# First batch of an attention and two-layer kernel: transposing unnormalized probabilities and scaling the product by spread reciprocal sums

## The chip, the cores and the metric

The kernel runs on one core of a Trainium2 chip. The metric is the device time of one execution in microseconds, the median of several; lower is better. A change of 0.2% (about 2.4 us here) is taken as the least that a measurement can tell from no change.

## What is computed

Attention over 4 batches of 12 heads, 448 positions, head size 64, with RMS-normalized q and k; its output, as 1792 tokens of 768 values, runs through two layers (768 to 2048 and back, twice).

```python
q_n, k_n = (rmsnorm(q, g_q), rmsnorm(k, g_k))
scores = scale * np.matmul(q_n, k_n.transpose(0, 1, 3, 2))
scores = scores - np.max(scores, axis=-1, keepdims=True)
attn = np.exp(scores)
attn = attn / (np.sum(attn, axis=-1, keepdims=True) + 1e-09)
return np.matmul(attn, v).astype(np.float32)
...
h = x @ w_in
g = h * (1.0 / (1.0 + np.exp(-1.702 * h)))
return (g @ w_out).astype(np.float32)
...
h = x @ w_in
g = np.maximum(h, 0.0) + alpha * np.minimum(h, 0.0)
return (g @ w_out).astype(np.float32)
```

The weight matrices arrive as 64-bit floats, read as pairs of 32-bit words; the other inputs have 32 bits. Most products are made of three fp16 products of a high and a low half each; in the first batch the product of probabilities and values is made in fp32 instead.

## The kernel before, in words

Two heads make a pair P, so a batch has 6 pairs, and a pair has 4 units u (three of 2 x 64 query rows for both heads, the last of 64 rows). `attention` walks over units with a lag: for each it computes the scores (`scores`, tile `sp`, six fp16 matmuls, then the row maximum `nm` on VectorE), the exponentials and their sums (`exponent`, tiles `pr` and `sm`), one step later `high`, two steps later `low`, and every second unit, four steps later, the product with the values (`values`, tile `xp`).

In the first batch (`u < 4 * NP`) `high` takes the reciprocal of the sums and makes with ScalarE for each of the unit's one or two row sets a diagonal matrix `dg` that holds them. `low` multiplies each 128-column piece of `pr` with `dg` on TensorE in fp32, which transposes and normalizes in one step (tile `tp` in PSUM), and ScalarE copies it to SBUF (`ptf`). `values` then multiplies `ptf` with the raw fp32 values `v`:

```python
dg = att_p.tile([128, 2, 128], F32, tag="ph", name="dg", bufs=PHB)
nc.scalar.activation(out=dg[:, i], in_=identf, func=AF.Copy, scale=sm[:, i:i + 1])
nc.tensor.matmul(out=tp[:, c, i], lhsT=pr[i][:, o:o + 128], rhs=ph[:, i], start=True, stop=True)
```

In the later batches the probabilities are normalized as two fp16 halves (`ph`, lines 505 and 531) and transposed by DMA; none of that is touched.

The order of the program: `first_pairs` runs the first two units of each pair of batch 0 (12 units, 256 of the 448 columns of x), while `w1i_steps` builds the first weight matrix from its words. Then `first_x` splits these 256 columns into halves, and the second two units of each pair run (12 units, 192 columns), interleaved with `first_in` on the first 256 columns (tile `hp`, line 651) and with `w1o_steps` for the second weight matrix. Then `first_moe1` runs `first_in` on the other 192 columns and `moe1_out` (tile `yp`, line 721), with batch 1's attention in between, and `moe1(1)` follows (line 698). Within this the tile framework's scheduler decides each engine's final order; engines run their instructions in that order and wait on semaphores. All DMAs are issued from SyncE's queue (SP), also in a fixed order. PSUM tiles `tp`, `hp`, `yp`, `pm` share three buffers of the pool `ps_m`; `xp` has one buffer of its own.

Lines named below: 393 to 410 and 424 normalize a pair's q and k, 429 transposes it by DMA (`t<-hl`), 148 to 165 and 179 to 180 build weights, 128 and 129 send a maximum through DRAM and back to all partitions (`line`, `row`), 307 and 308 read v for its largest value, 570 copies `xp` to `xraw`.

Of the kernel before, what the change touches and what calls it, by code (L numbers as in the profile page):

```python
# [9 lines left out]
F32 = mybir.dt.float32  # L10
# [3 lines left out]
AF = mybir.ActivationFunctionType  # L14
ALU = mybir.AluOpType
AX = mybir.AxisListType.X

EXP_MASK = 0x7F800000
EV = (True, True)
VN = 8  # L20
D1 = 2
RAW0 = 5
# [14 lines left out]
SQB = 2  # L37
HLB = 1
PHB = 3
# [18 lines left out]
def attention_moe_kernel(  # L58
# [17 lines left out]
    nc = tc.nc  # L76
    B, H, S, D = q.shape
# [4 lines left out]
    NP = H // 2  # L82
# [3 lines left out]
    NX = NX_  # L86

    const = ctx.enter_context(tc.tile_pool(name="const", bufs=1))
    big = ctx.enter_context(tc.tile_pool(name="big", bufs=1))
    dram = ctx.enter_context(tc.tile_pool(name="dram", bufs=1, space=bass.MemoryType.DRAM))  # L90
    small = ctx.enter_context(tc.tile_pool(name="small", bufs=2))
    work = ctx.enter_context(tc.tile_pool(name="work", bufs=2))
    ps_m = ctx.enter_context(tc.tile_pool(name="ps_m", bufs=3, space=bass.MemoryType.PSUM))
# [6 lines left out]
    identf = const.tile([128, 128], F32, name="identf")  # L100
# [37 lines left out]
    def split(dst, src, scale):  # L138

        nc.scalar.activation(out=dst[0], in_=src, func=AF.Copy, scale=scale)  # L140
        nc.vector.scalar_tensor_tensor(  # L141
            out=dst[1], in0=src, scalar=scale, in1=dst[0], op0=ALU.mult, op1=ALU.subtract
        )
# [116 lines left out]
    scales = {}  # L260
    loads = {}
    w1i = big.tile([128, KD, 2, FF], F16, tag="w", name="w1i", bufs=2)
# [5 lines left out]
    att_p = att.enter_context(tc.tile_pool(name="att_p", bufs=2))  # L268
# [6 lines left out]
    av = const.tile([128, B], F32, name="av")  # L275
# [170 lines left out]
    probs = {}  # L446
    pts = {}
    xs = {}
    xraw = {}
# [5 lines left out]
    FIRST = 256  # L455
    first_sc = const.tile([128, KD], F32, name="first_sc")

    def unit(u):

        P, r = divmod(u, 4)  # L460
        return (P, *UNITS[r])

    def scores(u):
# [15 lines left out]
        nc.scalar.activation(out=nm[:, 0:n], in_=nm[:, 0:n], func=AF.Copy, scale=c_s)  # L479
        probs[u] = (sp, nm, n)  # L480

    def exponent(u):
        sp, nm, n = probs[u]
        pr = [att_p.tile([128, S], F32, tag="p", name="pr", bufs=4) for _ in range(n)]
        sm = small.tile([128, 2], F32, tag="sm", name="sm", bufs=4)
        for i in range(n):
            nc.scalar.activation(  # L487
                out=pr[i], in_=sp[:, i, 0:S], func=AF.Exp, bias=nm[:, i:i + 1], scale=c_s, accum_out=sm[:, i:i + 1]
            )
        sm = sm[:, 0:n]  # L490
        nc.scalar.activation(out=sm, in_=sm, func=AF.Copy, scale=2.0 ** -14, bias=1e-9 * 2.0 ** -14)
        probs[u] = (pr, sm)

    def high(u):
        pr, sm = probs[u]
        nc.vector.reciprocal(out=sm, in_=sm)  # L496
        if u < 4 * NP:
            dg = att_p.tile([128, 2, 128], F32, tag="ph", name="dg", bufs=PHB)
            for i in range(len(pr)):
                nc.scalar.activation(out=dg[:, i], in_=identf, func=AF.Copy, scale=sm[:, i:i + 1])  # L500
            probs[u] = (pr, sm, dg)
            return
        ph = att_p.tile([128, 2, 2 * S], F16, tag="ph", name="ph", bufs=PHB)
        for i in range(len(pr)):
            nc.scalar.activation(out=ph[:, i, 0:S], in_=pr[i], func=AF.Copy, scale=sm[:, i:i + 1])  # L505
        probs[u] = (pr, sm, ph)

    def low(u):
        P, half, cols, place = unit(u)
        pr, sm, ph = probs.pop(u)  # L510
        n = len(pr)
        if u < 4 * NP:
            if (P, half) not in pts:
                pts[P, half] = att_p.tile([128, NV, 512], F32, tag="pt", name="ptf")
            for h in range(2):
                tp = ps_m.tile([128, 2, n, 128], F32, tag="m", name="tp")
                for c in range(2):
                    o = min(128 * (2 * h + c), S - 128)
                    for i in range(n):
                        nc.tensor.matmul(out=tp[:, c, i], lhsT=pr[i][:, o:o + 128], rhs=ph[:, i], start=True, stop=True)  # L520
                d = cols[1] - cols[0]
                to = pts[P, half][:, 2 * h:2 * h + 2, 0:2 * d].rearrange("p c (i t) -> p c i t", i=2)
                to = to[:, :, :, cols[0]:cols[0] + 64 * n]
                src = tp if n == 2 else tp.rearrange("p c n (i t) -> p c (n i) t", i=2)
                if EV[h]:
                    nc.scalar.activation(out=to, in_=src, func=AF.Copy)  # L526
                else:
                    nc.vector.tensor_copy(out=to, in_=src)
            return
        for i in range(n):  # L530
            nc.vector.scalar_tensor_tensor(  # L531
                out=ph[:, i, S:2 * S], in0=pr[i], scalar=sm[:, i:i + 1], in1=ph[:, i, 0:S], op0=ALU.mult, op1=ALU.subtract
            )
        if (P, half) not in pts:
            pts[P, half] = att_p.tile([128, 7, 512], F16, tag="pt", name="pt")
        for i in range(2):
            nc.sync.dma_start_transpose(  # L537
                out=pts[P, half][:, :, cols[i]:cols[i] + 64 * n], in_=ph[:, i] if n == 2 else ph[64 * i:64 * i + 64, 0]
            )

    def values(P, half):
        b, p = divmod(P, NP)
        vs = preps[P][1]
        pt = pts.pop((P, half))
        if half == 0 or b == 0:
            xps[P] = ps_x.tile([128, S], F32, tag="x", name="xp")
        xp = xps[P]
        if b == 0:
            steps = [(c, c, slice(64 if c == 3 else 0, 128)) for c in range(NV)]
        else:  # L550
            steps = [(c, c, slice(0, 128)) for c in range(7)] + [(c + 7, c, slice(0, 128)) for c in range(4)]
        parts = PARTS[half]
        for group in (parts,) if b else [(part,) for part in parts]:
            for i, (c, kc, ks) in enumerate(steps):
                for j, o, t, n in group:
                    nc.tensor.matmul(  # L556
                        out=xp[64 * j:64 * j + 64, t:t + n],
                        lhsT=vs[ks, j, c],
                        rhs=pt[ks, kc, o:o + n],
                        start=(i == 0),  # L560
                        stop=(i == len(steps) - 1),
                    )
        if b and half == 0:
            xs[b, p] = big.tile([128, 2, S], F16, tag="x", name="x", bufs=NX)
        elif b:
            x = xs[b, p]
            split((x[:, 0], x[:, 1]), xp, scales["w1i"][1][:, p:p + 1])
        elif half == 0:
            xraw[p] = big.tile([128, S], F32, tag="x", name="xraw", bufs=NX)
            nc.scalar.activation(out=xraw[p][:, 0:FIRST], in_=xp[:, 0:FIRST], func=AF.Copy)  # L570
        else:
            first_split(p, xp, slice(FIRST, S))

    def first_split(p, src, cols):
        x = xs[0, p]
        split((x[:, 0, cols], x[:, 1, cols]), src[:, cols], first_sc[:, p:p + 1])

    def first_x():
        nc.vector.tensor_scalar(out=first_sc, in0=scales["w1i"][1], scalar1=av[:, 0:1], scalar2=None, op0=ALU.mult)
        for p in range(NP):  # L580
            xs[0, p] = big.tile([128, 2, S], F16, tag="x", name="x", bufs=NX)
            first_split(p, xraw[p], slice(0, FIRST))
# [3 lines left out]
    def attention(us):  # L586

        for i in range(len(us) + LAG):
            if 0 < i <= len(us):
                high(us[i - 1])  # L590
            if i < len(us):
                scores(us[i])
                exponent(us[i])
            if 2 <= i <= len(us) + 1:
                low(us[i - 2])
            if i >= LAG and us[i - LAG] % 2 == 1:
                values(us[i - LAG] // 4, us[i - LAG] % 4 // 2)
            yield
# [304 lines left out]
    sums = {}  # L903
# [171 lines left out]
    if True:  # L1075
# [42 lines left out]
        for _ in w1i_steps:  # L1118
            pass
        v_scales(0, v0)  # L1120
        first_x()
        moe1_scales(0)
        for P in range(NP, NP + 2):
# [75 lines left out]
```

## Time and profile before

| | |
|---|---|
| time, median of 3 runs | 1196.87 us (1195.72 to 1196.92) |
| span of the profiled execution (first to last instruction) | 1199.3 us |
| TensorE matmul busy | 1086.5 us (91%) |
| VectorE busy | 822.6 us (69%) |
| ScalarE busy | 692.2 us (58%) |
| GpSimd busy | 80.1 us (7%) |
| mean granted TensorE clock | 0.970 |

The span is what the profile has as the profiled execution's own time; it stands 2.4 us above the median of the runs. Busy shares are averages over stages with different limits, so they have to be read stage by stage: the first hp matmul (line 651, 256 columns) starts at 140.5 us, the first of 192 columns at 222.1, the first yp at 289.7 and the first of batch 1's hp (line 698) at 367.1. A busy TensorE is not at its peak: where the granted clock is low the same matmul lasts longer.

### The profile page before, as it was taken

To read this page: it belongs to the slowest core of one execution; us is meant where nothing else is said; L and a number is where in the kernel's file an instruction comes from. 1 tells how busy PE (TensorE), PEld (TensorE's weight loads), DVE (VectorE), ACT (ScalarE), POOL (GpSimd) and SP (SyncE) were. 2 spreads that over 40 slices of the span, in tenths; PEclk is the share of its full clock that TensorE was granted. 3 is DMA by queue.
4 is the path that set the end of the run, shared out by engine and by line. 5 is a ranking of instruction groups with operands and counts; after the bars stand their busy time and mean duration, and the time that the engine had idled before them with its cause. 6 is when DMAs were issued, how large, how long until landed. Compare 5 with 4: busy or idle time off the path is not lost.

```text
span 1199.3 us, 18528 instructions
## 1 busy us (share of the span) xinstructions
PE 1086.5 (91%) x6826; PEld 612.5 (51%) x6826; DVE 822.6 (69%) x1445; ACT 692.2 (58%) x1425; POOL 80.1 (7%) x200
## 2 busy tenths in 40 slices
PE   0567899878998998999998999999999999999998
PEld 0335566655544444544554545544444467666665
DVE  6988889989567786457752677489995422977351
ACT  3877788877477776568852445346555422655220
POOL 3111000352101101010000000000000000000000
PEclk9887899978999999999998999999999999999999
DMA  7973555578587775645562741275614423353111
GB/s 216 272 175 109 144 159 148 114 157 171 117 152 143 139 152 118 149 97 115 106 142 57 263 139 51 78 262 176 219 71 149 141 75 126 97 161 109 34 27 33
DMA packets 267403, 160.82 MB, mean 134 GB/s; under 512 B 188592, under 2 KB 250672, under 8 KB 267312
## 3 DMA queue, kind: packets, MB, share of 16 engines
q1 hardware_dynamic: 267312, 159.64, 51.6%
q8 instruction: 53, 0.87, 0.3%
q14 instruction: 38, 0.31, 0.1%
HBM read 92.22 MB, written 25.69 MB: 98 GB/s over the span
## 4 chain that ended last, share of the span: by engine, by line
PE 44%; DVE 19%; ACT 14%; DMA 11%; issue 6%; SPq 4%; POOL 2%; ACTq 0%; DVEq 0%; POOLq 0%
PE op L983 16%; PE h L823 8%; PE yp L721 6%; PE hp L698 4%; ACT pr L487 4%; PE xp L556 4%; DVE ph L531 3%; PE hp L651 3%; DVE nm L478 3%; PE tp L520 3%; DMA t<-hl 2%; DMA yr<-y_dram 2%; ACT ph L505 2%; SPq L537 1%; PE sp L473 1%
## 5 line engine op out<-in xcount | busy, mean ns | idle before, releaser
L721 PE MATMUL yp<-g,w1o 128*128 128x448 f16 x1152 | 227.0, 355 | 4.3 <-ACT g L140 1.8
L823 PE MATMUL h<-x,w2i 128*128 128x512 f16 (+1 forms) x1152 | 219.3, 352 | 4.2 <-DVE pos L829 2.2
L698 PE MATMUL hp<-x,w1i 128*128 128x448 f16 x864 | 169.3, 353 | 2.6 <-DVE t L707 2.1
L721 PEld LDWEIGHTS <-w1o 128*128 128x128 f16 x1152 | 110.9, 98 | 116.6 <-issue 17.4
L823 PEld LDWEIGHTS <-w2i 128*128 128x128 f16 x1152 | 112.6, 98 | 109.9 <-issue 5.5
L698 PEld LDWEIGHTS <-w1i 128*128 128x128 f16 x864 | 82.2, 98 | 84.7 <-issue 10.4
L487 ACT ACTIVATE pr<-sp,nm,c_s 128x448 f32<-128x448 f32 x168 | 120.3, 719 | 4.4 <-PE tp L520 1.6
L531 DVE SCALAR_TENSOR_TENSOR ph<-pr,sm,ph 128x448 f16<-128x448 f32 x126 | 89.0, 731 | 20.3 <-ACT ph L505 20.3
L478 DVE TENSOR_REDUCE nm<-sp 128x2 f32<-128x896 f32 x96 | 92.3, 963 | 5.7 <-PE sp L473 5.7
L828 ACT ACTIVATE pos<-h,sign 128x512 f32<-128x512 f32 (+1 forms) x64 | 40.0, 627 | 86.6 <-PE h L823 80.2
L505 ACT ACTIVATE ph<-pr,sm 128x448 f16<-128x448 f32 x126 | 78.0, 660 | 18.9 <-DVE sm L496 18.8
L983 PEld LDWEIGHTS <-even 128*128 128x128 f16 x672 | 65.7, 98 | 43.4
L829 DVE SCALAR_TENSOR_TENSOR pos<-h,slope,pos 128x512 f32<-128x512 f32 (+1 forms) x64 | 43.4, 679 | 59.3 <-ACT pos L828 59.3
L473 PE MATMUL sp<-t 64*128 64x448 f16 (+1 forms) x480 | 62.2, 365 | 18.1 <-ACT pr L487 13.7
L651 PE MATMUL hp<-x,w1i 128*128 128x256 f16 (+1 forms) x576 | 66.0, 274 | 8.9 <-ACT ptf L526 3.3
L479 ACT ACTIVATE nm<-nm,c_s 128x2 f32<-128x2 f32 x96 | 27.7, 291 | 70.0 <-DVE nm L478 70.0
L520 PE MATMUL tp<-dg,pr 128*128 128x128 f32 x336 | 54.3, 322 | 14.1 <-ACT dg L500 14.1
L983 PEld LDWEIGHTS <-odd 128*128 128x128 f16 x504 | 49.3, 98 | 32.6
L651 PEld LDWEIGHTS <-w1i 128*128 128x128 f16 x576 | 55.4, 104 | 19.0 <-issue 14.9
L556 PE MATMUL xp<-pt,vs 128*64 128x256 f16 (+1 forms) x792 | 52.0, 279 | 12.7 <-DVE x L141 7.6
L983 PE MATMUL op<-w2lo,even 128*128 128x384 f16 x384 | 63.4, 326 | 0.0
L520 PEld LDWEIGHTS tp<-dg,pr 128*128 128x128 f32 x336 | 49.1, 230 | 23.5 <-ACT dg L500 15.9
(204 smaller groups left out, 1553.5 us busy)
## 6 DMA issues: line engine op xcount, KB each, us to landing
g<-in_moe_w_in_dram SPq DMA_DIRECT2D x24, 512.0 KB, 5.1
g<-in_moe_w_out_dram SPq DMA_DIRECT2D x32, 384.0 KB, 4.0
w2raw<-in_moe_w_in_dram SPq DMA_DIRECT2D x24, 512.0 KB, 5.7
w2raw<-in_moe_w_out_dram SPq DMA_DIRECT2D x16, 768.0 KB, 6.6
g_dram<-pos SPq DMA_DIRECT2D x48, 256.0 KB, 2.0
gp<-g_dram SPq DMA_DIRECT2D x8, 1024.0 KB, 6.7
odd<-g_dram SPq DMA_DIRECT2D x6, 1024.0 KB, 5.6
y_dram<-y SPq DMA_DIRECT2D x24, 224.0 KB, 2.3
```

What stands on the lines that cost most here:

```text
L473: nc.tensor.matmul(out=sp[:, j, 0:S] if n == 2 else sp[ds, 0, 0:S], lhsT=qt[ds] if n == 2 else qt[ds, 64:128], rhs=kt[ds, 0:S], start=(i = ...
L478: nc.vector.tensor_reduce(out=nm[:, 0:n], in_=sp[:, 0:n, 0:S], op=ALU.max, axis=AX, negate=True)
L487: nc.scalar.activation(out=pr[i], in_=sp[:, i, 0:S], func=AF.Exp, bias=nm[:, i:i + 1], scale=c_s, accum_out=sm[:, i:i + 1])
L505: nc.scalar.activation(out=ph[:, i, 0:S], in_=pr[i], func=AF.Copy, scale=sm[:, i:i + 1])
L520: nc.tensor.matmul(out=tp[:, c, i], lhsT=pr[i][:, o:o + 128], rhs=ph[:, i], start=True, stop=True)
L531: nc.vector.scalar_tensor_tensor(out=ph[:, i, S:2 * S], in0=pr[i], scalar=sm[:, i:i + 1], in1=ph[:, i, 0:S], op0=ALU.mult, op1=ALU.subtract)
L556: nc.tensor.matmul(out=xp[64 * j:64 * j + 64, t:t + n], lhsT=vs[ks, j, c], rhs=pt[ks, kc, o:o + n], start=(i == 0), stop=(i == len(steps) ...
L651: nc.tensor.matmul(out=ps, lhsT=w1i[:, kk, e, m * 128:(m + 1) * 128], rhs=xs[0, kk][:, f, cols], start=(i == 0), stop=(i == 3 * KD - 1))
L698: nc.tensor.matmul(out=ps, lhsT=w1i[:, kk, e, m * 128:(m + 1) * 128], rhs=x[:, f], start=(n == 0), stop=(n == 3 * KD - 1))
L721: nc.tensor.matmul(out=ps, lhsT=w1o[:, m, e, j * 128:(j + 1) * 128], rhs=g[:, m, f], start=(n == 0), stop=(n == 3 * KF - 1))
L823: nc.tensor.matmul(out=ps, lhsT=w2i[:, kk, e, m * 128:(m + 1) * 128], rhs=x2[kk][:, f], start=(c == 0), stop=(c == 3 * KD - 1))
L983: nc.tensor.matmul(out=ps, lhsT=ops[:, o, m, f], rhs=rhs[:, e], start=(c == 0), stop=(c == 3 * KH - 1))
```

## The change

In the first batch `exponent` keeps the sums of two units side by side in one tile `sums`, and after the second adds 1e-9 and takes the reciprocal on VectorE; the scaling of the sums on ScalarE and the diagonal matrices are gone. `low` transposes `pr` as it is with TensorE's transpose against the identity. After the second unit `spread_sums` multiplies the reciprocals, broadcast over 64 columns, with the identity (fp32), which gives them along the free axis and over the 64 partitions of each head (tile `rp`); ScalarE copies that to SBUF (`own`, in the first half the tile `xraw` itself). `values` multiplies its product in PSUM with `own` on VectorE. For the second half the split into halves then reads SBUF.

```diff
+        if u < 4 * NP:
+            if u % 2 == 0:
+                sums_of[P, half] = small.tile([128, 4], F32, tag="sums", name="sums", bufs=3)
+            sm = sums_of[P, half][:, 2 * (u % 2):2 * (u % 2) + n]
...
-        nc.scalar.activation(out=sm, in_=sm, func=AF.Copy, scale=2.0 ** -14, bias=1e-9 * 2.0 ** -14)
+        if u >= 4 * NP:
+            nc.scalar.activation(out=sm, in_=sm, func=AF.Copy, scale=2.0 ** -14, bias=1e-9 * 2.0 ** -14)
+        elif u % 2:
+            sm = sums_of[P, half][:, 0:2 + n]
+            nc.vector.tensor_scalar(out=sm, in0=sm, scalar1=1e-9, scalar2=None, op0=ALU.add)
+            nc.vector.reciprocal(out=sm, in_=sm)
...
+    def spread_sums(P, half):
+        rs = sums_of.pop((P, half))
+        rp = ps_m.tile([128, 256], F32, tag="m", name="rp")
+        for h in range(2):
+            hs = slice(64 * h, 64 * h + 64)
+            for r in range(2):
+                if r and half:
+                    nc.tensor.matmul(
+                        out=rp[hs, 128:192], lhsT=rs[hs, 2:3].to_broadcast([64, 64]), rhs=identf[hs, hs], start=True, stop=True
+                    )
+                else:
+                    nc.tensor.matmul(
+                        out=rp[hs, 128 * r:128 * r + 128], lhsT=rs[:, 2 * r + h:2 * r + h + 1].to_broadcast([128, 64]),
+                        rhs=identf, start=True, stop=True
+                    )
+        if half:
+            own = att_p.tile([128, S - FIRST], F32, tag="sq", name="own", bufs=SQB)
+        else:
+            xraw[P] = big.tile([128, S], F32, tag="x", name="xraw", bufs=NX)
+            own = xraw[P][:, 0:FIRST]
+        nc.scalar.activation(out=own, in_=rp[:, 0:S - FIRST] if half else rp, func=AF.Copy)
+        spread[P, half] = own
...
-        if u < 4 * NP:
-            dg = att_p.tile([128, 2, 128], F32, tag="ph", name="dg", bufs=PHB)
-            for i in range(len(pr)):
-                nc.scalar.activation(out=dg[:, i], in_=identf, func=AF.Copy, scale=sm[:, i:i + 1])
-            probs[u] = (pr, sm, dg)
-            return
...
-                        nc.tensor.matmul(out=tp[:, c, i], lhsT=pr[i][:, o:o + 128], rhs=ph[:, i], start=True, stop=True)
+                        nc.tensor.transpose(out=tp[:, c, i], in_=pr[i][:, o:o + 128], identity=identf)
...
+            if u % 2:
+                spread_sums(P, half)
             return
...
-            xraw[p] = big.tile([128, S], F32, tag="x", name="xraw", bufs=NX)
-            nc.scalar.activation(out=xraw[p][:, 0:FIRST], in_=xp[:, 0:FIRST], func=AF.Copy)
+            own = spread.pop((P, 0))
+            nc.vector.tensor_tensor(out=own, in0=xp[:, 0:FIRST], in1=own, op=ALU.mult)
         else:
-            first_split(p, xp, slice(FIRST, S))
+            own = spread.pop((P, 1))
+            cols = slice(FIRST, S)
+            nc.vector.scalar_tensor_tensor(
+                out=own, in0=xp[:, cols], scalar=first_sc[:, p:p + 1], in1=own, op0=ALU.mult, op1=ALU.mult
+            )
+            x = xs[0, p]
+            nc.scalar.activation(out=x[:, 0, cols], in_=own, func=AF.Copy)
+            nc.vector.tensor_tensor(out=x[:, 1, cols], in0=own, in1=x[:, 0, cols], op=ALU.subtract)
```

The scheduler puts much of the first 370 us into another order. Three places follow; the lines of the changed kernel are its own (there 495 is the exponential, 147 the step of line 148, 556 the copy to ptf, 526 the copy of rp).

ScalarE at the second and third unit, before and then changed (`w1i` and `g_139` are weights and their words):

```order
L487 ACTIVATE pr,sm<-sp,nm,c_s 128x448 x2
L500 ACTIVATE dg<-identf,sm 128x128 x2
L148 ACTIVATE w1i<-g_139 128x512
L423 ACTIVATE hl<-qk 128x896
L491 ACTIVATE sm<-sm 128x2
L391 ACTIVATE sq<-qk 128x448 x2
L148 ACTIVATE w1i<-g_139 128x512
L479 ACTIVATE nm<-nm,c_s 128x2
L526 ACTIVATE ptf<-tp 128x4x128
```

```order
L147 ACTIVATE w1i<-g_139 128x512 x2
L556 ACTIVATE ptf<-tp 128x4x128
L478 ACTIVATE nm<-nm,c_s 128x2
L556 ACTIVATE ptf<-tp 128x4x128
L178 ACTIVATE w1i<-w1i,inv_w1i 128x2048
L495 ACTIVATE pr,sums<-sp,nm,c_s 128x448 x2
```

The first copy to `ptf` stood behind the second unit's exponentials and the diagonals; it now stands ahead of the second unit's exponentials.

SyncE's queue where the last pair of batch 0 is transposed (`t_548` before, `t_538` changed), before and then changed:

```order
L223 DMA g_139<-in_moe_w_in_dram 128x1024 x2
L128 DMA line_7466<-am 128x1
L129 DMA row<-line_7466 128x128
L223 DMA g_139<-in_moe_w_out_dram 128x4x192
L429 DMA_TRANSPOSE t_548<-hl 128x14x128
L307 DMA vst<-in_v_dram 128x336 x4
L223 DMA g_139<-in_moe_w_out_dram 128x4x192
L307 DMA vst<-in_v_dram 128x336 x4
L223 DMA g_139<-in_moe_w_out_dram 128x4x192 x18
L429 DMA_TRANSPOSE t_2017<-hl 128x14x128
```

```order
L222 DMA g_139<-in_moe_w_in_dram 128x1024
L428 DMA_TRANSPOSE t_538<-hl 128x14x128
L222 DMA g_139<-in_moe_w_in_dram 128x1024
L306 DMA vst<-in_v_dram 128x336 x2
L127 DMA line_7448<-am 128x1
L128 DMA row<-line_7448 128x128
L222 DMA g_139<-in_moe_w_out_dram 128x4x192
L306 DMA vst<-in_v_dram 128x336 x2
L222 DMA g_139<-in_moe_w_out_dram 128x4x192
L306 DMA vst<-in_v_dram 128x336 x4
L222 DMA g_139<-in_moe_w_out_dram 128x4x192 x30
L440 DMA vs<-vs 64x2x192
```

The transpose of the last pair passed the send of the maximum `am`; the first transpose of batch 1 (`t_2017` before) now stands behind all loads of the second weight matrix.

VectorE where the first pair's product is taken out of PSUM in the changed kernel (before, ScalarE did that, line 570):

```order
L164 SCALAR_TENSOR_TENSOR w1i<-g_139,w1i 128x512 x3
L602 TENSOR_TENSOR xraw<-xp,xraw 128x256
L423 TENSOR_TENSOR hl<-qk,hl 128x896
L295 TENSOR_REDUCE vone<-v_95 128x1
L392 TENSOR_REDUCE ss<-sq 128x7
L477 TENSOR_REDUCE nm<-sp 128x2
```

The multiplication by `own` stands on VectorE ahead of the third pair's normalization and the next row maximum.

## Rows read from the trace of the kernel before

**Rows 1.** Busy time by stretch: length, then each engine's busy us and (instructions), clock, DMA

```profile
core 0: us, PE busy (x) PEld busy (x) DVE busy (x) ACT busy (x) POOL busy (x), PEclk, DMA share, GB/s
...
30.00:140.50 110.50, 76.80 (x402) 50.06 (x403) 95.53 (x180) 84.50 (x198) 14.11 (x42) 0.85 0.65 179
140.50:222.10 81.60, 78.20 (x580) 55.45 (x579) 72.96 (x164) 68.75 (x173) 1.37 (x1) 1.00 0.61 151
222.10:289.70 67.60, 49.03 (x493) 38.37 (x493) 60.51 (x120) 55.44 (x134) 29.86 (x41) 0.85 0.72 138
289.70:367.10 77.40, 72.56 (x488) 36.90 (x488) 49.49 (x92) 46.11 (x111) 8.63 (x29) 0.98 0.69 144
```

**Rows 2.** Waits from 30 to 140.5 us: waiter, releaser, us in total, times, longest

```profile
PE tp L520 <- ACT dg L500: 14.1, 5, 4.6
ACT xraw L570 <- PE xp L556: 13.4, 6, 5.9
...
PE sp L473 <- ACT w1i L148: 8.6, 1, 8.6
...
DVE g L164 <- ACT g L148: 5.4, 1, 5.4
...
PE sp L473 <- DMA t<-hl: 4.5, 1, 4.5
...
DVE vcol L308 <- DMA vst<-in_v_dram: 2.4, 1, 2.4
...
DVE a L134 <- DMA row<-line: 1.7, 1, 1.7
```

**Rows 3.** SyncE's queue in order of time: start, us, issue

```profile
89.99 0.33 SPq L128 DMA_DIRECT2D line<-am  x1
97.92 0.33 SPq L129 DMA_DIRECT2D row<-line  x1
...
98.82 3.78 SPq L429 DMA_TRANSPOSE t<-hl  x1
```

**Rows 4.** Groups of equal instructions, 0 to 367.1 us: busy us, mean ns, idle before

```profile
L500 ACT ACTIVATE dg<-identf,sm 128x128 f32<-128x128 f32 x42 | 14.5, 397 | 0.5 <-DVE rm_w1i L105 0.5
...
L491 ACT ACTIVATE sm<-sm 128x2 f32<-128x2 f32 x38 | 7.7, 203 | 0.2
...
L663 DVE SCALAR_TENSOR_TENSOR g<-t,hp 128x256 f32<-128x256 f32 x16 | 6.4, 412 | 2.0 <-ACT t L662 1.5 <-DMA g<-in_moe_w_out_dram 0.5
...
L140 ACT ACTIVATE x<-xp,first_sc 128x192 f16<-128x192 f32 x6 | 2.6, 425 | 2.5 <-PE xp L556 2.5
...
L663 DVE SCALAR_TENSOR_TENSOR g<-t,hp 128x192 f32<-128x192 f32 x5 | 1.7, 340 | 0.0
```

**Rows 5.** The same view, the instructions of normalizing a pair and the row maximum

```profile
L478 DVE TENSOR_REDUCE nm<-sp 128x2 f32<-128x896 f32 x39 | 42.1, 1080 | 5.7 <-PE sp L473 5.7
...
L393 DVE TENSOR_REDUCE ss<-sq 128x7 f32<-128x448 f32 x36 | 21.1, 611 | 12.6 <-ACT sq L391 12.6
...
L410 DVE TENSOR_TENSOR qk<-qk,rs 128x896 f32<-128x896 f32 x12 | 12.6, 1087 | 9.0 <-POOL rs L404 8.8
...
L424 DVE TENSOR_TENSOR hl<-qk,hl 128x896 f16<-128x896 f32 x11 | 11.9, 1082 | 0.6 <-ACT hl L423 0.6
...
L409 DVE TENSOR_TENSOR qk<-qk,gs 128x512 f32<-128x512 f32 x14 | 9.6, 684 | 0.0
```

**Rows 6.** TensorE in order of time: start, us, instructions merged

```profile
47.16 3.78 PE L520 MATMUL tp<-dg,pr 128*128 128x128 f32 x16 [4.65 <-ACT dg L500]
...
56.63 2.05 PE L520 MATMUL tp<-dg,pr 128*128 128x128 f32 x16
...
165.42 2.14 PE L651 MATMUL hp<-x,w1i 128*128 128x256 f16 x18
167.49 0.74 PE L473 MATMUL sp<-t 64*128 64x448 f16 x6
```

**Rows 7.** Busy time of the instructions on tile tp, second stretch: length, PE, PEld, ACT

```profile
140.50:222.10 81.60, 18.39 (x128) 15.58 (x128) 10.30 (x22) 1.00 0.61 151
```

More of the change, by code (lines that the diff above doesn't have):

```diff
@@ L18 @@
 EXP_MASK = 0x7F800000
-EV = (True, True)
 VN = 8
@@ L480, in scores @@
         probs[u] = (sp, nm, n)
+    sums_of = {}
+    spread = {}
     def exponent(u):
         sp, nm, n = probs[u]
+        P, half, _, _ = unit(u)
         pr = [att_p.tile([128, S], F32, tag="p", name="pr", bufs=4) for _ in range(n)]
-        sm = small.tile([128, 2], F32, tag="sm", name="sm", bufs=4)
+        if u < 4 * NP:
[3 more added lines that the diff above has]
+        else:
+            sm = small.tile([128, 2], F32, tag="sm", name="sm", bufs=4)[:, 0:n]
         for i in range(n):
@@ L489, in exponent @@
             )
-        sm = sm[:, 0:n]
-        nc.scalar.activation(out=sm, in_=sm, func=AF.Copy, scale=2.0 ** -14, bias=1e-9 * 2.0 ** -14)
-        probs[u] = (pr, sm)
+        if u >= 4 * NP:
[4 more added lines that the diff above has]
+            nc.vector.reciprocal(out=sm, in_=sm)
+        probs[u] = (pr, sm)
+    def spread_sums(P, half):
[15 more added lines that the diff above has]
+            own = att_p.tile([128, S - FIRST], F32, tag="sq", name="own", bufs=SQB)
+        else:
+            xraw[P] = big.tile([128, S], F32, tag="x", name="xraw", bufs=NX)
+            own = xraw[P][:, 0:FIRST]
+        nc.scalar.activation(out=own, in_=rp[:, 0:S - FIRST] if half else rp, func=AF.Copy)
+        spread[P, half] = own
     def high(u):
+        if u < 4 * NP:
+            return
         pr, sm = probs[u]
         nc.vector.reciprocal(out=sm, in_=sm)
-        if u < 4 * NP:
-            dg = att_p.tile([128, 2, 128], F32, tag="ph", name="dg", bufs=PHB)
-            for i in range(len(pr)):
-                nc.scalar.activation(out=dg[:, i], in_=identf, func=AF.Copy, scale=sm[:, i:i + 1])
-            probs[u] = (pr, sm, dg)
-            return
         ph = att_p.tile([128, 2, 2 * S], F16, tag="ph", name="ph", bufs=PHB)
@@ L509, in low @@
         P, half, cols, place = unit(u)
-        pr, sm, ph = probs.pop(u)
-        n = len(pr)
         if u < 4 * NP:
+            pr, _ = probs.pop(u)
+            n = len(pr)
             if (P, half) not in pts:
@@ L524, in low @@
                 src = tp if n == 2 else tp.rearrange("p c n (i t) -> p c (n i) t", i=2)
[L525 to L528, printed above, removed]
+                nc.scalar.activation(out=to, in_=src, func=AF.Copy)
+            if u % 2:
+                spread_sums(P, half)
             return
+        pr, sm, ph = probs.pop(u)
+        n = len(pr)
         for i in range(n):
@@ L578, in first_x @@
     def first_x():
-        nc.vector.tensor_scalar(out=first_sc, in0=scales["w1i"][1], scalar1=av[:, 0:1], scalar2=None, op0=ALU.mult)
+        nc.vector.tensor_scalar(
+            out=first_sc, in0=scales["w1i"][1], scalar1=av[:, 0:1], scalar2=2.0 ** 14, op0=ALU.mult, op1=ALU.mult
+        )
         for p in range(NP):
```

## The prediction, on record before the run

> **What bounds the kernel now.** I first cut the span by what TensorE begins: the second half of the first batch's attention from 140.5 us, the 192-column hp matmuls from 222.1, yp from 289.7, batch 1's hp from 367.1. The order of the changed kernel has all of batch 0 and batch 1 in the same amount ahead of that last mark (52 units of attention scored in both), and the same pattern behind it. The 832 us behind it hold none of the changed instructions, so the change is worth what it moves the mark at 367.1 us. The view of busy time by stretch [rows 1] shows a different limit in each. From 30 to 140.5 us VectorE is the fullest (95.5 of 110.5 us, 15.0 idle); TensorE is busy 76.8 us at a granted clock of 0.85, and waits. From 140.5 to 222.1 TensorE is full: 78.2 of 81.6 at full clock. From 222.1 to 289.7 VectorE is full again (60.5 of 67.6), and from 289.7 to 367.1 TensorE (72.6 of 77.4). The view of waits then says what the first of these stages waits for [rows 2]: TensorE 14.1 us for the diagonals, ScalarE 13.4 us at the copy of xp, and VectorE 5.4 us for a weight step that stands behind that copy on ScalarE.
>
> **ScalarE's part.** 42 diagonals go, 14.5 us; 24 scalings of the sums go, 24 x 0.203 = 4.9 [rows 4]. The six copies of xp become six copies of rp of the same size, nothing; six copies of rp for the second half come new, 6 x 0.425 = 2.6. So 16.8 us less work, but ScalarE is not the fullest engine in any of the four stretches, so I count nothing for that by itself. It also takes the reciprocal, the diagonal and their waits out of the way from the exponential to the transpose; the 14.1 us belong to TensorE, which is not the bound there, so again nothing by itself.
>
> **VectorE's part.** 24 reciprocals become 12 additions and 12 reciprocals of as few elements: even. Six multiplications of 256 columns out of PSUM come new in the first stage; no row has this instruction, the nearest is line 663 with the same columns and PSUM source, 0.412 us: 2.5 us. In the second stage the subtraction of 192 columns replaces nothing (the other two steps of the split stay, the copy to halves on ScalarE too): bounded by line 663 at 192 columns, 6 x 0.340 = 2.0 [rows 4].
>
> **First stage, 30 to 140.5.** By the order, VectorE does the same work before it as now, but for the normalization of one pair that goes behind it: 4 sums of squares, 2 and 2 multiplications, 1 subtraction [rows 5], 4 x 0.611 + 2 x 0.684 + 2 x 1.087 + 1.082 = 7.1 us. It moves into a stretch where TensorE is the bound and VectorE has 8.6 us to spare [rows 1]. With the 2.5 added, VectorE's work falls by 4.6. Of its 15.0 us idle, 2.4 + 1.7 = 4.1 stand behind the send of a maximum through DRAM [rows 2]: SP issues line at 89.99, waits for it until 97.92, and only then transposes the last pair [rows 3]. The order puts that transpose ahead of the send, so its scores (TensorE waited 4.5 us for them) come earlier and I drop the 4.1. What waits 7.9 us for the row instead is loads of v and of the second weight matrix, two of whose buffers are filled ahead. The 5.4 us behind the xp copy I keep: VectorE now waits for xp itself. Sum -4.6 - 4.1 = **-8.7 us**; the stage ends at 131.8. Bounds: it loses if VectorE waits more for xp (rival 1), and gains up to the rest of the idle time, 15.0 - 4.1 = 10.9 us more, if the shorter way from exponential to xp removes that too.
>
> **Second stage, 140.5 to 222.1.** TensorE is the bound, so its work counts in full. 64 of the 168 fp32 products for tp lie here: 128 records, 18.4 us [rows 7]. Back to back at full clock 16 records (8 products) take 2.05 us, 0.256 us a product [rows 6]. No row has an fp32 transpose. Below I bound it by one pass of 128 columns at the rate of hp, 18 of 256 columns in 2.14 us, so 0.059; above by the product as it is, 0.256. I take one of the two records, 0.128, since the data and columns are those of the product: 64 x 0.128 = 8.2, 10.2 less. The six spreads add 12 fp32 products of 128 columns and 12 of 64 columns: 12 x 0.256 + 12 x 0.128 = 4.6. By the order five units of scores (30 matmuls, 0.74 us for six [rows 6], 3.7 us) leave the stage. Sum **-9.3 us**; with the bounds of the transpose -1.1 to -13.7. VectorE keeps up: 73.0 + 7.1 + 2.0, less the row maxima of five units (about 5 us by 1.080 each [rows 5]), is 77, above the 72.3 us that would be left for TensorE, so part of the gain can be held back by up to 4.8; against that, batch 1's first fp16 halves leave the stage too, so I leave the term.
>
> The Trainium skill (TensorE: Matmul & The Clock Gate, section Part 4: PE-mode transpose) gives a transpose of 128 x 128 about 275 ns within a kernel, more than the product's 256 here; by it the 64 would take 17.6 us and the stage would lose 0.1. The page's measurement is of bf16, and no row here shows a transpose on TensorE.
>
> **Third and fourth stage.** The order now has 34 units scored at the first yp instead of 41, but 52 at the mark in both: seven units (five of the second stage, two of the third) go into the fourth. Together the two last 145.0 us with 110.0 of VectorE, 101.6 of ScalarE and 121.6 of TensorE [rows 1], which the five units' scores raise to 125.3. No engine is full over both, so I add the scores, **+3.7 us**, and no gain for the better spread.
>
> **The sum.** -8.7 - 9.3 + 3.7 = -14.3. Against the profiled execution that is 1199.3 - 14.3 = 1185.0 us of span; its span stands 2.4 above the median of the runs, so I forecast **1182.6 us**, 1.2% faster.
>
> **Rivals.**
> 1. *VectorE waits at the product.* It now stands in order at six multiplications for xp, where ScalarE stood 13.4 us [rows 2]. If all of that reaches VectorE, 13.4 - 5.4 = 8.0 are added: 1190.6. For it: xp comes after the spread's copy on ScalarE. Against: transposes start without diagonals, so xp is earlier. Chance 0.18.
> 2. *The units pushed behind the second stage.* Batch 1's first transpose stands behind all loads of the second weight matrix. If 28 units (24 to 52) go at the 5.6 us of the third stage (67.6 us [rows 1] for 12 units by the order), they take 158 us, 13 more than 145, 9.1 beyond the 3.7 counted: 1191.7; with half of the first stage's gain missed too, 1196, no change that can be told. Chance 0.13, half of it within 0.2%.
> 3. *The clock, slower than before.* In the first stage TensorE has 0.85 of its clock at 76.8 us busy [rows 1]; at the lower level the same 16 records took 3.78 instead of 2.05 us [rows 6]. Its work there falls: 108 scores x 0.123, 104 transposes x 0.128, 48 values' products of 256 columns x 0.512 and 24 spreads x 0.256 make 57.3 us at 2.4 GHz. If with so much less to do it stays at 1.2 GHz throughout, that is 114.6 us, and with the 8.6 and 4.5 us that it waits for others in any case [rows 2] the stage ends at 30 + 127.7 = 157.7, 25.9 later than forecast: 1208.5. It decides from a mean clock under 57.3 / (101.8 - 13.1) = 0.65. Against it: dense runs of the spread, transposes and values follow one another. Chance 0.09. The same section of the skill says that the full clock does not engage for transposes, which would make this rival likelier; no row shows one.
> 4. *The transpose is no faster than the product* (the change does not do that part): the second stage gains 1.1, 1190.8. Chance 0.06.
>
> **How the numbers follow.** The forecast has 0.54, and its own range is 1167 to 1188: below by 10.9 of idle time and 4.4 of a cheaper transpose, above by a VectorE-bound second stage. The range 1167 to 1197 takes in rivals 1, 2 and 4 and leaves out rival 3 and a tenth at the edges. Faster by over 0.2% (about what a measurement can tell): the forecast, 1, 4 and half of 2, less some for what the scheduler's other order may cost elsewhere, 0.83; within 0.2% 0.07; slower 0.10.
>
> **What would show it.** Right: the first 256-column hp matmul near 132 us, the first 192-column one near 204, batch 1's first hp near 353, and nothing changed after; transposes at 0.13 us back to back; no wait of scores for t<-hl near 100 us. Wrong: VectorE idle before the multiplication by own for over 10 us in sum (rival 1); over 148 us from the 192-column hp to batch 1's hp (rival 2); a granted clock under 0.65 from 30 to 132 us (rival 3); transposes at 0.25 us (rival 4).

## The result: slower by 0.5%, and the profile after

| | before | changed |
|---|---|---|
| time, median, us | 1196.9 | 1204.1 |
| ratio to before, 95% interval | | 1.0051 [1.0031, 1.0072] |
| span of the profiled execution, us | 1199.3 | 1204.3 |

The forecast was 1182.6 us, its range ended at 1197, and slower had a chance of 0.10. Lines of the changed kernel: 692 is `first_in`'s hp (651 before), 762 yp (721), 739 batch 1's hp (698), 551 tp, 517 and 513 rp, 390 the squares `sq` (391), 428 `t<-hl` (429), 606 the multiplication of the second half by `own`, 611 the last reading of `own`.

Busy time by stretch of the changed kernel, cut at the same marks as [rows 1], with what lies behind batch 1's first hp as a last row:

```profile
30.00:128.90 98.90, 65.78 (x347) 33.50 (x348) 90.60 (x177) 72.64 (x152) 8.74 (x28) 0.91 0.72 190
128.90:208.68 79.78, 76.11 (x533) 52.34 (x533) 69.07 (x162) 57.88 (x129) 1.72 (x5) 0.96 0.46 134
208.68:266.00 57.32, 41.17 (x396) 32.29 (x393) 51.75 (x102) 43.82 (x105) 23.98 (x45) 0.85 0.56 114
266.00:367.10 101.10, 86.15 (x618) 42.93 (x618) 71.72 (x124) 69.15 (x167) 16.73 (x34) 0.97 0.78 152
367.10:731.40 364.30, 341.61 (x2234) 174.29 (x2233) 229.53 (x393) 225.23 (x498) 18.95 (x56) 0.98 0.59 133
```

The first yp starts 23.7 us earlier than before (266.0 against 289.7), and all of that is gone at batch 1's first hp: 367.1 us in both. In the third and fourth stage TensorE is busy 127.3 us of 158.4; before, 121.6 of 145.0. It waits there, and this says for what (waits of TensorE from 208.68 to 367.1 us):

```profile
PE sp L472 <- ACT pr L495: 16.1, 9, 5.2
...
PE xp L588 <- DMA pt<-ph: 9.5, 7, 2.9
```

The same two waits in the kernel before, from 222.1 to 367.1 us:

```profile
PE sp L473 <- ACT pr L487: 9.0, 4, 5.8
PE xp L556 <- DMA pt<-ph: 3.6, 4, 2.2
```

The two grew by 13.0 us; other waits shrank, so that of the 13.4 us that these stages are longer 7.7 are idle time of TensorE and 5.7 work that moved there. Both are attention of batch 1: scores that find no free buffer, products that wait for the transposed probabilities. That attention starts late. SyncE's queue of the changed kernel has the transposes of batch 1's first two pairs at 217.5 and 224.2 us; before, they stood at 169.6 and 181.6.

```profile
217.46 2.79 SPq L428 DMA_TRANSPOSE t<-hl  x1
...
224.16 1.55 SPq L428 DMA_TRANSPOSE t<-hl  x1
```

One step further back lies the cause. The squares with which the normalization of these two pairs begins were computed at 68 and 91 us in the kernel before (ScalarE in order of time):

```profile
68.13 1.03 ACT L391 ACTIVATE sq<-qk 128x448 f32<-128x448 f32 x2
...
90.68 1.04 ACT L391 ACTIVATE sq<-qk 128x448 f32<-128x448 f32 x2
```

In the changed kernel the first of them runs at 196:

```profile
196.15 0.59 ACT L390 ACTIVATE sq<-qk 128x448 f32<-128x448 f32 x1
...
198.83 0.58 ACT L390 ACTIVATE sq<-qk 128x448 f32<-128x448 f32 x1
```

That is 1.9 us after VectorE has read pair 4's `own` for the last time (VectorE in order of time; the second row is pair 5's):

```profile
193.93 0.35 DVE L611 TENSOR_TENSOR x<-own,x 128x192 f16<-128x192 f32 x1
...
205.30 0.35 DVE L611 TENSOR_TENSOR x<-own,x 128x192 f16<-128x192 f32 x1
```

The diff has the reason in one word: `own` of the second half is taken with `tag="sq"`, so it shares the two buffers of the squares. Six tiles of `own` stand ahead of pair 6's squares there, and the last two go back only at 194.3 and 205.7 us, when batch 0's attention ends. The four squares of the two pairs now stand in rows of one (x1, before x2): each starts after the sum over the one before it, which fits a single buffer while pair 5's `own` holds the other. I call this **the tie**.

Rows 7 have their answers in the busy time of tile tp and, new, of tile rp in the second stage (length, TensorE, weight loads, ScalarE):

```profile
128.90:208.68 79.78, 10.62 (x64) 7.28 (x64) 10.32 (x22) 0.96 0.46 134
```

```profile
128.90:208.68 79.78, 8.57 (x48) 5.00 (x48) 1.95 (x6) 0.96 0.46 134
```

The transposes took 18.4 - 10.6 = 7.8 us off TensorE [rows 7], and the spread put 8.6 on.

### The profile page after: what moved, and what is told of

Same layout as the page of the kernel before. It is cut to its first block, busy times and chain, and to the rows that moved or that the text cites. A ratio compares the mean times of both kernels' runs of the same rounds, so it can differ in the third digit from the quotient of the medians.

```text
span 1204.3 us, 18349 instructions
## 1 busy us (share of the span) xinstructions
PE 1078.1 (90%) x6754; PEld 592.4 (49%) x6754; DVE 828.8 (69%) x1457; ACT 682.4 (57%) x1365; POOL 79.5 (7%) x200
## 4 chain that ended last, share of the span: by engine, by line
PE 38%; DVE 21%; DMA 13%; ACT 13%; issue 7%; SPq 5%; POOL 3%; ACTq 0%; POOLq 0%; DVEq 0%
PE op L1024 16%; PE h L864 8%; PE yp L762 5%; ACT pr L495 4%; PE hp L739 3%; DMA qk<-in_q_dram 3%; DVE nm L477 3%; DVE ph L563 2%; PE xp L588 2%; DMA t<-hl 2%; PE hp L692 2%; ACT ph L536 2%; SPq L569 2%; DMA w2raw<-in_moe_w_in_dram 1%; DMA yr<-y_dram 1%
## 5 line engine op out<-in xcount | busy, mean ns | idle before, releaser
L588 PEld LDWEIGHTS <-vs 128*64 128x64 f16 x792 | 39.7, 115 | 31.0 <-issue 16.9
L139 ACT ACTIVATE g<-t,ratio_w1o 128x448 f16<-128x448 f32 x64 | 42.1, 662 | 21.2 <-DVE t L748 19.7
```

What stands on the lines that cost most here:

```text
L588: nc.tensor.matmul(out=xp[64 * j:64 * j + 64, t:t + n], lhsT=vs[ks, j, c], rhs=pt[ks, kc, o:o + n], start=(i == 0), stop=(i == len(steps) ...
```

## The experiments

Two questions: is the tie the cause, and where would the forecast gain be without it? Each ratio is to runs of the kernel before made together with it (medians 1199.0 to 1199.8 us there).

**e1, the tie removed.**

```diff
-            own = att_p.tile([128, S - FIRST], F32, tag="sq", name="own", bufs=SQB)
+            own = att_p.tile([128, S - FIRST], F32, tag="ph", name="own", bufs=PHB)
```

> The second half's own is put into the buffers of tag ph (which dg used before) instead of the two of tag sq; nothing else differs. Theory A (the tie): own of pairs 4 and 5 holds both sq buffers until VectorE has read it at 194 and 205.7 us, so the squares of batch 1's first two pairs, next in the same rotation, start at 216.9 instead of before 170, and from there to batch 1's second stage attention is what is late. Then here t<-hl of pair 6 returns from 217.5 to 155-170 us, batch 1's first hp comes at 350-358 us, and the time is 1180-1190. Theory B (the units are late for the changed engines' load, the buffer is no matter): 1200-1206, batch 1's first hp at 365 or later. Theory C (something behind that first hp costs the 6 us, in the time after it 837 us instead of 832): the first hp earlier, but the time behind it still 836-838.

Measured: 1198.8 us, ratio 0.9999 [0.9985, 1.0014]. SyncE's queue has pair 6 back in its old place:

```profile
169.12 1.51 SPq L428 DMA_TRANSPOSE t<-hl  x1
```

The 0.5% are gone, and behind batch 1's first hp (366.9) stand 830.5 us, so the 5 us lost there went with the tie too, and theory C falls. But the gain that A promised did not come: the time is that of before. (The 216.9 us in the expectation were misread: they are pair 8's squares in the kernel before. In the changed kernel pair 6's start at 196.)

**e2, the tie alone, in the kernel before.**

```diff
+            if u % 2 and half:
+                tie[P] = att_p.tile([128, S - FIRST], F32, tag="sq", name="tie", bufs=SQB)
+                nc.gpsimd.memset(tie[P][:, 0:1], 0.0)
...
             first_split(p, xp, slice(FIRST, S))
+            nc.gpsimd.tensor_copy(out=tie.pop(P)[:, 0:1], in_=xs[0, p][:, 1, FIRST:FIRST + 1])
```

> The kernel before with the tie alone: a tile of tag sq is taken after each pair's second half of tp and given back after the split of x, with a memset and a copy of one column on GpSimd, 12 tiny instructions; all else stays, diagonals and products too. A: pairs 6 and 7 are transposed behind all 32 loads of the second weight matrix as in the changed kernel, near 220 us or later; the time rises by about what the tie costs the changed kernel, 14-24 us, to 1211-1221. B: within 3 us of before, 1194-1200.

Measured: 1205.4 us, 1.0057 [1.0038, 1.0077]. ScalarE and SyncE show the changed kernel's delay in a kernel that has none of its other parts:

```profile
195.37 0.58 ACT L391 ACTIVATE sq<-qk 128x448 f32<-128x448 f32 x1
```

```profile
213.80 1.58 SPq L429 DMA_TRANSPOSE t<-hl  x1
```

Taken away and put in by itself, the tie is worth the same 0.5 to 0.6%: shown in both directions, though my 14 to 24 us were too much. Each of the two edits also gives the scheduler another order, hundreds of rows of it; that the same squares and transposes move both times, and the time by the same amount, speaks for the tie and against chance.

**e3, TensorE's saving taken back** (on e1, as all of e3 to e5, e7 to e9, e11 and e13 to e16).

```diff
-                        nc.tensor.transpose(out=tp[:, c, i], in_=pr[i][:, o:o + 128], identity=identf)
+                        nc.tensor.matmul(out=tp[:, c, i], lhsT=pr[i][:, o:o + 128], rhs=identf, start=True, stop=True)
```

> As e1, but tp is made by an fp32 product with the identity (two records of 0.128 us at full clock) and not by the transpose (one). If the second stage is bound by TensorE as the prediction has it, 64 x 0.128 = 8.2 us more than e1 (6 to 11 with the first stage's share); if the transposes' speed is hidden, within 2 us of e1, and the gain came from the diagonals that are gone.

Measured: 1199.0 us, 1.0004 [0.9988, 1.0019], the same as e1. The second stage, e1's and then e3's (columns of [rows 1]):

```profile
133.30:221.71 88.41, 82.23 (x564) 54.35 (x564) 73.89 (x169) 65.57 (x155) 0.29 (x1) 0.92 0.52 140
```

```profile
131.30:218.96 87.66, 85.16 (x627) 60.33 (x627) 75.76 (x175) 67.18 (x158) 1.28 (x1) 1.00 0.55 147
```

e3 executes 63 records more in 0.8 us less (a product is two records, a transpose one): its clock is 1.00, e1's 0.92. Rows of 5 us show where e1 loses it:

```profile
145.00:150.00 5.00, 3.90 (x34) 3.02 (x33) 5.00 (x14) 5.00 (x13) 0.00 (x0) 1.00 0.27 84
150.00:155.00 5.00, 2.44 (x16) 0.84 (x13) 3.63 (x8) 2.20 (x5) 0.00 (x0) 0.89 0.79 235
155.00:160.00 5.00, 4.61 (x18) 2.68 (x19) 4.91 (x13) 3.54 (x11) 0.00 (x0) 0.50 0.17 39
```

TensorE is busy for half of the second row, waiting for ScalarE's copy to `ptf`; in the third row the granted clock is 0.50, that is 1.2 GHz, and 18 records take 4.6 us where the first row has 34 in 3.9. e3 has no such gap there. So in e1 part of what the transposes save is lost in a gap, and in the lower clock behind it. How much the other order of e3 adds, this run cannot say (below).

**e4, the spread left out.**

```diff
-            nc.vector.tensor_tensor(out=own, in0=xp[:, 0:FIRST], in1=own, op=ALU.mult)
+            nc.vector.tensor_scalar(out=own, in0=xp[:, 0:FIRST], scalar1=2.0 ** -8, scalar2=None, op0=ALU.mult)
```

(and likewise in the second half, with rp's products and copies gone)

> As e1, but the reciprocal sums are not spread and not multiplied in: no rp on TensorE, no copy of rp on ScalarE, and VectorE takes xp times a constant at the same place (the probabilities of batch 0 stay unnormalized). The prediction's price: 4.6 us of rp in the second stage and none in the first, so 3-6 us below e1. If the spread's wait chain (sums, rp, its copy, the multiplication) is what costs: 8 us or more below e1.

Measured: 1196.6 us, 0.9984 [0.9967, 1.0002]: 2 us below e1. The second stage ends 8.9 us earlier (212.8 against 221.7), but the third then takes 77.1 us, with VectorE 70.7 of them busy, where e1's took 64.2.

**e5 and e6, three pairs' normalization on GpSimd**, on e1 and on the kernel before.

```diff
-        return nc.gpsimd if NP + 2 <= P < 2 * NP else nc.vector
+        return nc.gpsimd if 3 <= P < NP or NP + 2 <= P < 2 * NP else nc.vector
```

> As e1, but the two multiplications and the subtraction that normalize q and k of pairs 3 to 5 stand on GpSimd instead of VectorE: 3 x (0.68 + 1.09 + 1.08) = 8.5 us less for VectorE before 130 us; the rest is as it was. Theory D (VectorE, with the second weight matrix and the attention in its queue, limits everything up to about 240-290 us; TensorE is full in the second stage only with work that it could do later): batch 1's first yp and hp come 4-8 us earlier and the time is 1191-1195. Theory E (a chain that VectorE is not in fixes the third pair of batch 1 near 240 us): within 2 us of e1, 1197-1200.

> The kernel before with the same move of pairs 3 to 5 to GpSimd. D: 2-8 us faster than before, 1189-1195, and if VectorE is no longer the limit then, TensorE's second stage begins to count and e5 is ahead of this by 2-8 us. E: within 2 us of before.

Measured: 1.0036 [1.0016, 1.0056] and 1.0018 [0.9995, 1.0041]. Neither theory foresaw e5's loss; its trace has a new wait in the first stage, a small product put ahead in TensorE's order whose input VectorE makes late:

```profile
PE pm L119 <- DVE diag L117: 15.9, 1, 15.9
```

So e5 says nothing on VectorE's work.

**e7, VectorE given more.**

```diff
         nc.vector.tensor_reduce(out=nm[:, 0:n], in_=sp[:, 0:n, 0:S], op=ALU.max, axis=AX, negate=True)
+        if u < 4 * NP and u % 4 > 1:
+            nc.vector.tensor_reduce(out=nm[:, 0:n], in_=sp[:, 0:n, 0:S], op=ALU.max, axis=AX, negate=True)
```

> As e1, but VectorE takes the row maximum of each of the 12 units of batch 0's second half twice: 6 x (1.0 + 0.54) = 9.2 us more for it from 125 to 222 us, and nothing for TensorE or ScalarE but the wait. D: the time rises by 6-10 us over e1, to 1205-1209. If TensorE or the loads bind there (E): by at most 3 us.

Measured: 1208.6 us, 1.0073 [1.0046, 1.0101], 9 us over e1, as D had it.

**e8, the third pair's load set free.**

```diff
-            if j == KF - 2:
+            if j >= KF - 2:
```

> As e1, but the last row block of the second weight matrix is staged in a buffer of tag ph, not of tag qk, so the load of q and k of batch 1's third pair no longer waits for it (216 us in e1; its transpose at 239.7). E: that transpose comes 20 us or more earlier, the units up to batch 1's first hp follow, and the time is 1185-1193. D: the transpose comes earlier and the time stays within 2 us of e1, as VectorE takes the units no sooner.

Measured: 1208.5 us, 1.0074 [1.0048, 1.0099]. The transpose came at 223.8 instead of 239.7 us, as wanted, and the time rose by 9 us: both theories miss it, E outright.

**e9 and e10, VectorE given less**, on e1 and on before: the shift of the second weight matrix's words left out.

> As e1, and the shift of the second weight matrix's words is left out on VectorE (32 instructions of 0.35 us, 11.2 us less for it from 115 to 222 us; the second weight matrix has other values then). No other engine has less to do. Theory D (VectorE limits this part, so that TensorE's and ScalarE's savings lie idle): 5-11 us below e1, 1188-1194. Theory E (VectorE's 9.2 us of e7 cost what they did by another order only): within 2 us of e1.

> The kernel before with the same shifts left out. D: faster than before, but TensorE, with 10 us more to do than in e9, comes to bind, so by less than in e9: 1190-1195 and e9 ahead of this by 2-8 us. If both gain the same, the change has nothing to give in this stage even where VectorE has room.

Measured: 1.0000 [0.9983, 1.0018] and 1.0024 [1.0010, 1.0039]. 11 us less for VectorE gain nothing, in e10 they lose. D as I had it falls.

**e11 and e12, the first two pairs of batch 1 on GpSimd** (`NP <= P < 2 * NP`), on e1 and on before.

> As e1, with the normalization of batch 1's first two pairs on GpSimd, as it already is for the four after them: 2 x 2.85 = 5.7 us less for VectorE from 145 to 205 us, where GpSimd is idle. D: 2-6 us below e1, 1193-1197, ahead of before too. E: within 2 us of e1, or slower by the longer way to the transposes.

> The kernel before with the same move. D: 0-5 us below before, less than e11 gains on e1.

Measured: 1.0037 [1.0024, 1.0051] and 1.0006 [0.9989, 1.0023]: no gain again.

**e13 and e14, two reliefs at once.**

> The omissions of e4 (no spread of the sums; batch 0 stays unnormalized) and e9 (no shift of the second weight matrix's words) together on e1: TensorE has some 9 us less and VectorE 11 us less to do from 130 to 222 us. Theory F (the two engines bind this stretch in turn, so that either relief alone is caught by the other): the sum is worth more than its parts, 6-12 us below e1, 1187-1193. Theory G (what is gained before the first yp is lost behind it, whatever is relieved): 1195-1198, no more than e4 had.

> The identity product of e3 with e9's omission: TensorE is kept at full clock from 130 to 222 us (1.00 in e3, 0.93 in e1) and has 8 us more to do than in e9, VectorE 11 us less than in e3. F: no better than e3 within 2 us, as TensorE then binds. G: the same. If it is 4 us or more below e3, VectorE alone binds where TensorE keeps its clock, and the lower clock of e9 is what hid that.

Measured: 0.9962 [0.9946, 0.9978], 1194.0 us, and 1.0017 [0.9998, 1.0036]. In e13 both reliefs together give 5 us, against the 2 and 0 that they gave apart. 1194 lies between the ranges of F and G, and the intervals of e13 and e4 overlap, so this does not decide; and 20 us of work were left out.

The engines' orders tell why these results do not fit together. Against e1, each of e3 to e5 and e7 to e9 differs in hundreds of rows of TensorE's order and of VectorE's, only a small part of them the edit itself: the scheduler makes a new order for each of these edits. e5, e8 and e11 lose 0.4 to 0.7% where work was only moved or a load set free. So none of them is a clean measure of one cost.

**e15, the spread made cheaper at the same order.** Its four products of a second half are issued shape by shape instead of head by head; VectorE's, ScalarE's and SyncE's orders are those of e1 row for row, and TensorE's differs in these products alone.

```diff
-        for h in range(2):
-            hs = slice(64 * h, 64 * h + 64)
-            for r in range(2):
+        for r in range(2):
+            for h in range(2):
+                hs = slice(64 * h, 64 * h + 64)
```

> As e1, but the spread's four products of a pair's second half are issued shape by shape (the two of 128 columns, then the two of 64) instead of head by head. In the changed kernel the four equal products of a first half take 0.66 us, the four of a second half in turn 1.30 us. If the turns between shapes are what costs, a second half takes 0.6 to 0.8 us here, 3-4 us less for TensorE in the second stage in all (rp 9.3 to 5.5-6); by e4 (which left out all of the spread and ended 2 us earlier) the time falls by no more than 1.5 us: 1197-1199. If each product has its own price, 1.2-1.3 us as in e1 and the time the same.

Measured: 1194.6 us, 0.9959 [0.9942, 0.9976]: **faster than both kernels**, by more than I expected. One pair's spread on TensorE, in e1 and then in e15:

```profile
169.38 0.43 PE L517 MATMUL rp<-identf,sums 128*64 128x128 f32 x2
169.74 0.32 PE L513 MATMUL rp<-identf,sums 64*64 64x64 f32 x2
170.00 0.43 PE L517 MATMUL rp<-identf,sums 128*64 128x128 f32 x2
170.36 0.32 PE L513 MATMUL rp<-identf,sums 64*64 64x64 f32 x2
```

```profile
163.72 0.44 PE L517 MATMUL rp<-identf,sums 128*64 128x128 f32 x4
164.09 0.33 PE L513 MATMUL rp<-identf,sums 64*64 64x64 f32 x4
```

1.30 us became 0.70, with the same eight records. The rows say how: in e15 the four records of a shape, two products, together last as long as the two records of one product in e1 (0.44 and 0.43, 0.33 and 0.32). The products of the two heads write different halves of the partitions; shape by shape they run side by side, their records 6 ns apart in the trace. Head by head, a product of the other shape stands between them, and they follow one another. In the second stage tile rp fell from 9.3 to 4.8 us, and the stage with it (e15):

```profile
132.80:215.59 82.79, 77.41 (x564) 51.70 (x564) 73.45 (x169) 65.72 (x155) 0.17 (x1) 0.95 0.55 150
...
279.60:361.20 81.60, 71.12 (x489) 36.32 (x488) 50.23 (x94) 45.64 (x109) 8.44 (x28) 1.00 0.68 146
```

It is 5.6 us shorter than e1's, batch 1's first hp comes 5.7 us earlier (361.2 against 366.9), and so does the end (span 1191.7 against 1197.4; the medians differ by 4.2). G falls: with the order held, what TensorE saves in the second stage reaches the end here. That e4, with no spread at all, was 2 us slower than this (the intervals overlap) can be its order.

**e16, the same on e3.**

> The same reordering on e3 (fp32 product with the identity in place of the transpose), where TensorE kept its full clock in the second stage and was full: 3-4 us less work there. 1196-1199; a version ahead of before would be at 1196 or less.

Measured: 1197.5 us, 0.9988 [0.9974, 1.0001]. Every engine's order is that of e3 but for products on tile xp and rp of TensorE, so this is a second pair at one order. Its second stage, beside e3's above:

```profile
131.60:216.51 84.91, 81.59 (x627) 58.26 (x627) 75.53 (x175) 66.66 (x158) 1.28 (x1) 1.00 0.56 150
```

Tile rp fell from 7.8 to 4.5 us and the stage by 2.7, but the median by only 1.4, and the intervals overlap. So that such a saving reaches the end whole is shown for e1 and not for e3; where e16 loses it I have not traced. The transpose is worth 3 us against the identity product here (e15 against e16) and nothing in e1 against e3, each time at other orders.

**e17, the same with the tie.**

> The changed kernel itself (own in the sq buffers) with the spread's products issued shape by shape as in e15; every engine's order is else the same as before this edit. If what TensorE saves in the second stage reaches the end as it did from e1 to e15 (4.6 us of rp, about 4 us of time), 1198-1201. If the tie leaves TensorE's second stage off the path, since batch 1's attention comes late in any case, within 1.5 us of the changed kernel, 1203-1206.

Measured: 1204.5 us, 1.0042 [1.0025, 1.0058]: no different from the changed kernel. Tile rp fell to 4.9 us here too, but

```profile
129.40:208.02 78.62, 74.04 (x534) 50.69 (x533) 68.77 (x162) 57.63 (x129) 1.72 (x5) 0.93 0.47 135
```

the stage is only 1.2 us shorter, and batch 1's first hp starts at 367.0 as it did. That fits the second of the two expectations, that the tie takes TensorE's second stage off the path. The two faults do not add up: the spread's price costs 0.4% without the tie and, within the noise, nothing with it. Why the stage itself is not shorter by more with the tie I have not traced.

## Why the prediction was wrong, point by point

Against before the stages are 98.9 - 110.5 = -11.6, 79.8 - 81.6 = -1.8, 158.4 - 145.0 = +13.4 and, behind batch 1's first hp, 837.2 - 832.2 = +5.0: +5.0 in all, where I summed -14.3. The first stage came out 2.9 us better than its term; the gain of the second fell 7.5 us short, the loss of the third and fourth was 9.7 us larger, and what lies behind the mark had been put at nothing.

- **First stage, -8.7: size nearly right, reason wrong.** The term of 7.1 us, "the normalization of one pair that goes behind it", was the step that failed. I read in the order that the squares went behind the mark and counted that as a gain, since they would find room there. I did not ask what had moved them. It was the tie, and it moved them by more than 100 us. VectorE's work in the stage did fall, by 4.9 us where I had 4.6; the price of what was moved stands in the later stages. In e1 they are back in the first stage, and this still ends 7.2 us earlier than before: VectorE is idle for 6.3 us of its 103.3 there instead of 15.0, which I had listed only as a bound.
- **Second stage, -9.3: two terms mis-sized.** The 64 transposes saved 7.8 us and not 10.2; the spread cost 8.6 and not 4.6. I priced the spread's products by an fp32 product of equal columns [rows 6], one after the other; at full clock a spread of a second half takes 1.30 us where I had 0.77, and shape by shape 0.70 (e15). The scores left as said, but by the tie's doing: 24 units are scored at the end of the stage with it, 29 before and in e1 and e15. With that, TensorE's work in the stage fell by about 3 us, of which the clock (0.96 instead of 1.00) took its part.
- **Third and fourth stage, +3.7.** "No engine is full over both, so I add the scores": wrong, for what counts there is when attention may start. Rival 2 had the mechanism and the length, 158 us; 158.4 were measured. I gave it 0.13, and its time of 1191.7 came too low because the gain of the second stage in it did not exist and 5 us more were lost behind it.
- **"The change is worth what it moves the mark at 367.1 us"**: TensorE's order behind the mark is the same, yet 837 us stand there in the changed kernel and e17, 833.7 in e2, and 830.5 in e1 and e15. At an equal count of scored units attention can still be behind: the transpose of the 15th pair comes at 378.8 us in the changed kernel, 379.6 in e2 and 379.2 in e17, all behind that mark, but at 365.3 before, 366.1 in e1 and 360.5 in e15, ahead of it. The mark itself is the same with the tie and without (367.1 and 366.9 in e1), so what the tie costs in the changed kernel appears behind it; in e2 most of it is there at the mark already (369.9).
- **Rival 1** did not happen: VectorE waited 0.4 us for xp at the multiplication in the first stage, which the rival was about, and 4.9 in the second. **Rival 3**: the first stage's clock was 0.91. **Rival 4**: eight transposes in a row took 1.04 us at full clock, 0.13 each, as I had it. The Trainium skill (TensorE: Matmul & The Clock Gate, section Part 4: PE-mode transpose) has about 275 ns for one within a kernel; this trace has half of that in such runs.
- What was right, without the tie: TensorE bounds the second stage, and a saving there shortens it (e15, e16); in e15 it reaches the end. The change does win, 0.4%, once its two faults are out.
- **Even so it is 5 us and not 14.** e15's second stage is 1.2 us longer than before (82.8 against 81.6), not 9.3 shorter. No scores leave it; the transposes there save 7.6 us and the spread costs 4.8, but TensorE's busy time falls by only 0.8 (77.4 against 78.2), at a clock of 0.95 instead of 1.00, and it waits more.

Open: where e16 loses what it saves; what a relief of VectorE alone would bring at a fixed order (e9 and e11 changed that too), and how much of e3's equality with e1 is the clock and how much its order.

## What to carry to other kernels

When a change takes a tile from an existing pool, list who else rotates through that tag, and when: a tile that is held long makes every later user of the tag wait, across phases and engines, and a step that the new order has far later than before is a question to answer, not a gain to count. Where a scheduler orders the program, measure a cost with an edit that leaves the order as it is, and compare the orders before trusting the time; here setting one load free cost 0.7%. Group small products by shape, so that those that write different partitions can run side by side.

## What the runs showed of the hardware that had not been expected

- **Side by side, or in turn, on TensorE.** Four fp32 products of 128 by 64 rows and columns and 128 columns of output, two for each head, take 0.66 us (the spread of a first half, changed kernel):

```profile
62.41 0.66 PE L517 MATMUL rp<-identf,sums 128*64 128x128 f32 x8
```

Two of these and two smaller ones of 64*64 in turn take 1.30 us at full clock, the same four shape by shape 0.70 to 0.79 (e15). Most of that is overlap: shape by shape, the two heads' products of one shape last no longer than one. The Trainium skill (TensorEngine Tiling (Array Packing), section Key Properties) says that changing the tiling mode drains TensorE, while different tiles run in parallel. The trace agrees with the second (0.44 us for two products, 0.43 for one); the price of a change of mode by itself no run here separates. By that rule the spread's price could have been doubted ahead.
- **A lower clock behind a gap.** In e1, behind 5 us with TensorE busy for 2.44, the granted clock was 0.50 for the next 5 us; over the whole second stage the kernels in which tp is still a product, with more work for TensorE, were granted 0.98 to 1.00 (before, e2, e3, e6, e10, e12, e14, e16), those with transposes 0.90 to 0.99. Their orders differ too, so that the transposes lower the clock is not shown.
